# Scoring a key block in one burst of eight matmuls, with one ring of eight PSUM banks for all users

## The chip, the core and the metric

The kernel runs on one core of one Trainium2 chip. The core has a matrix engine (TensorE, called PE in the profile, with its weight loads shown apart as PEld), VectorE (DVE), ScalarE (ACT), GpSimd (POOL), and a queue that only issues transfers (SyncE, SP). PE writes its results to PSUM, which has eight banks; one bank holds 512 fp32 values in each of 128 partitions. ACT and DVE read the banks and write to on-chip memory (SBUF). The metric is the device time of one execution in microseconds, where less is better; the figure given is the median of the runs.

## What is computed

Two parts follow each other. First comes attention over 4 batches, 8 heads, 768 positions and a head size of 64, where each query sees the first 4 keys (the sinks) and the last 128 keys. Then comes a gated feed-forward network (FFN) over all 3072 tokens, 512 wide, with 1536 hidden units and an RMS norm ahead of it. Cut to what matters:

```python
def _attn_ref(q, k, v, n_sink, window):          # B=4, H=8, S=768, D=64, n_sink=4, window=128
    scores = np.matmul(q, k.transpose(0, 1, 3, 2)) / np.sqrt(D)
    keep = (pos[None, :] < n_sink) | ((rel >= 0) & (rel < window))   # rel = query position - key position
    a = softmax(np.where(keep, scores, -1e9))
    return np.matmul(a, v)

def _moe_ref(x, w_gate, w_val, w_out, rms_g):    # x: 3072 x 512, d_ff = 1536
    xn = x / np.sqrt(np.mean(x * x, axis=-1, keepdims=True) + 1e-6) * rms_g
    g = xn @ w_gate
    return (g / (1 + np.exp(-g)) * (xn @ w_val)) @ w_out
```

## The kernel before

The 3072 tokens are 24 blocks of 128, numbered g; block g is position t = g mod 6 of batch b = g div 6. Four blocks make a group G of 512 tokens for the FFN. A key block t is seen by the queries of blocks t and t+1 alone, so the scores are made by key block: for each head one matmul with 128 keys held as weights and 256 queries passing (128 queries at t = 5, the last block of a batch). A head has 64 rows, so these are 64-row matmuls. Two heads, a head pair, stand in the two halves of the 128 rows; a block has four head pairs.

Blocks 0, 1 and 3 are scored by another routine (`unit_bias` and `unit_sp`, L341 and L358): a 128-row matmul first writes the mask into the bank, and eight 64-row matmuls of 128 queries add the scores. The other 21 blocks (2 and 4 to 23) go through `unit_s(g, u)` (L380), called twice for each block. A call scores two head pairs: four 64-row matmuls (L389) into the tile `pT`, which is two banks wide and of which there is one; one exponential on ACT over both banks (L396); and the mask, on DVE (L409) for the first two batches and every first block of a batch, else on POOL (L411, L416). `unit_av(g, u)` (L430) then multiplies the masked exponentials with the values for four heads into a bank `pv`; DVE divides by the sum (L472, L477), ACT squares and sums (L487), and DVE makes the RMS factor and the scaled row `xr` (L496 to L534).

`unit_t1` and `unit_t` (L256, L272) turn queries and keys through PE and a copy on ACT or DVE (from block 12 on, DMAs on SP do it, except for a batch's first block). `unit_x` (L546) does the same for `xr` of the first eight blocks. `unit_sink` and `unit_sink_scores` (L291, L316) do the four sink keys. The FFN is cut into parts: a gate part (four 512-column matmuls into `pg`, then tanh on ACT, L587), a value part (four into `pvl`, then two products on DVE, L592 and L600), and output parts (four each into `po`, three to a bank, then a copy on ACT, L622, and a store from SP). In group 0 a gate or value part is eight matmuls of 256 columns.

The order on PE and SP is the order of the code. `step(g)` (L629) lays the attention work of a block into four slots, and `weave` (L652) deals the slots out between the FFN parts; the first slots of the weave are written by hand (L717 to L729). After the prologue the order on ACT, DVE and POOL is chosen when the program is built, by a scheduler that plans with estimated times. PSUM after the prologue has three rings: `b1` with four banks (FFN, transposes, sinks), `pv` with two (AV), and `pT` with its two. A tile takes the bank of its ring that comes free next in the scheduler's plan, and its first matmul waits on the chip until that bank's last reader is done.

Of the kernel before, what the change touches and what calls it, by code (L numbers as in the profile page):

```python
# [9 lines left out]
ALU = mybir.AluOpType  # L10
ACT = mybir.ActivationFunctionType
FP32 = mybir.dt.float32
BF16 = mybir.dt.bfloat16
# [15 lines left out]
def kernel(  # L29
# [311 lines left out]
    def unit_bias(g, n):  # L341

        if PROLOGUE[0]:
            banks = [pp[0].tile([P, 512], FP32, name="ph", tag="ph", bufs=6)
                     for hi in range(2)]
        else:
            pT = pp[0].tile([P, 2, 512], FP32, name="pT", tag="pT", bufs=1)
            banks = [pT[:, hi, :] for hi in range(2)]
        for hi in range(2):
            nc.tensor.matmul(  # L350
                out=banks[hi].rearrange("p (x c) -> p x c", c=P), lhsT=ident,
                rhs=amasks[:, 0 if g % NT == 0 else 1, n, :].unsqueeze(1).to_broadcast(
                    (P, HP, P)),
                start=True, stop=False, skip_group_check=True,
            )
        PTS[(g, n)] = banks
# [20 lines left out]
            for hp in range(HP):  # L377
                E[(g, 2 * hp + hi, n)] = et[:, hp, :]

    def unit_s(g, u):  # L380
        b, t = divmod(g, NT)
        nq = 2 if t + 1 < NT else 1
        w = nq * P
        pT = pp[0].tile([P, 2, 512], FP32, name="pT", tag="pT", bufs=1)
        for j in range(2):
            hp = 2 * u + j
            for hi in range(2):
                pr = slice(hi * D, (hi + 1) * D)
                nc.tensor.matmul(  # L389
                    out=pT[:, hi, j * 256:j * 256 + w],  # L390
                    lhsT=QKT[b][pr, 1, hp, t * P:(t + 1) * P],
                    rhs=QKT[b][pr, 0, hp, t * P:t * P + w],
                    start=True, stop=True,
                )
        et = epool.tile([P, 4, 2, P], BF16, name="et")
        nc.scalar.activation(  # L396
            out=et[:, :, 0:nq, :].rearrange("p x n c -> p x (n c)"),
            in_=pT.rearrange("p i (j c) -> p (i j) c", c=256)[:, :, 0:w],
            func=ACT.Exp, scale=inv_sqrt_d,
        )  # L400
        if b < POOL_MASK_FROM or t == 0:
            m = masks[:, 0 if t == 0 else 1, 0:nq, :]
            if nq == 2:
                ev = et.rearrange("p x n c -> p x (n c)")
                mv = m.rearrange("p n c -> p (n c)").unsqueeze(1).to_broadcast((P, 4, w))
            else:
                ev = et[:, :, 0, :]
                mv = m.to_broadcast((P, 4, P))
            nc.vector.tensor_tensor(out=ev, in0=ev, in1=mv, op=ALU.mult)  # L409
        else:  # L410
            nc.gpsimd.affine_select(  # L411
                out=et[:, :, 0, :], in_=et[:, :, 0, :], compare_op=ALU.is_ge,
                fill=0.0, base=0, pattern=[[0, 4], [1, P]], channel_multiplier=-1,
            )
            if nq == 2:
                nc.gpsimd.affine_select(  # L416
                    out=et[:, :, 1, :], in_=et[:, :, 1, :], compare_op=ALU.is_ge,
                    fill=0.0, base=-1, pattern=[[0, 4], [-1, P]],
                    channel_multiplier=1,
                )  # L420
        for j in range(2):
            for hi in range(2):
                for n in range(nq):
                    E[(g, 4 * u + 2 * j + hi, n)] = et[:, 2 * hi + j, n, :]

    def halves(g):

# [2 lines left out]
    def unit_av(g, u):  # L430
        b, t = divmod(g, NT)

        pv = pp[0].tile(
            [P, 512], FP32, name="pv", tag="b1" if PROLOGUE[0] else "pv", bufs=2
        )
        if t >= 2:
            nc.tensor.matmul(  # L437
                out=pv[:, 0:HW], lhsT=ESK[(b, t)],
                rhs=VSK[b][:, 4 * u:4 * u + 4, :],
                start=True, stop=False, skip_group_check=True,  # L440
            )
# [223 lines left out]
    with tc.manual_schedule(engines=MANUAL_ALL):  # L665
# [18 lines left out]
        for u in range(2):  # L684
# [16 lines left out]
        )  # L701
        pools.close()
        pp[0] = ctx.enter_context(
            tc.tile_pool(name="psum", bufs=4, space=bass.MemoryType.PSUM)
        )
        PROLOGUE[0] = False

    with tc.manual_schedule(engines=MANUAL):
# [6 lines left out]
        for ft in range(FA, FTN):  # L715
            fb += parts_f(0, (ft,), slice(0, GN))
        weave(fa, [  # L717
            [lambda: unit_t1(2, 1), lambda: unit_bias(1, 1), lambda: unit_sp(1, 1), lambda: unit_sink(0)],
            [lambda: unit_t1(3, 0), lambda: unit_s(2, 0)],
            [lambda: unit_s(2, 1), lambda: unit_sink_scores(0, 2)],  # L720
            [lambda: unit_t1(3, 1), lambda: unit_bias(3, 0), lambda: unit_av(2, 0), lambda: unit_sp(3, 0), lambda: unit_av(2, 1)],
            [lambda: unit_av(3, 0)],
            [lambda: unit_av(3, 1), lambda: unit_t1(4, 0)],
# [2 lines left out]
            [lambda: unit_t1(4, 1)],  # L726
            [lambda: unit_x(3)],
        ], first=True)
        slots = [[lambda: unit_t1(5, 0)], [lambda: unit_s(4, 0), lambda: unit_t1(5, 1)], [lambda: unit_s(4, 1)], [lambda: unit_sink_scores(0, 4)], [lambda: unit_t(6)], []]  # L729
        for g in range(5, NB + 3):  # L730
            slots += step(g)
        slots[6].pop()
# [51 lines left out]
```

## Time and profile before

| | |
|---|---|
| time, median of 3 runs | 261.87 us (261.83, 261.87, 262.98) |
| span of the profiled execution, first to last instruction | 259.7 us |
| median of the runs less that span | 2.2 us |
| instructions in the profile | 4764 |
| PEld, DVE, ACT, POOL busy | 125.8, 180.3, 138.3, 96.6 us |
| mean granted TensorE clock | 0.997 |
| HBM read, written | 28.31 MB, 6.29 MB |

Of the profiled execution only the span is given and no time of its own, so its time is taken as the span and the 2.2 us by which the median of the runs exceeds it. PE's busy time includes the modelled tails of pipelined matmuls, which overlap: a 512-column matmul is shown as 0.379 us, but eight in a row advance by 0.216 us each. How far PE has got is therefore read from the starts of instructions in the timeline and not from busy time. The idle time that the timeline shows in brackets is given with what ended it. Some matmul records are missing (278 of 288 `po` matmuls are there), which shows as an x7 where eight matmuls stand.

### The profile page before, as it was taken

To read this page: it belongs to the slowest core of one execution; us is meant where nothing else is said; L and a number is where in the kernel's file an instruction comes from. 1 tells how busy PE (TensorE), PEld (TensorE's weight loads), DVE (VectorE), ACT (ScalarE), POOL (GpSimd) and SP (SyncE) were. 2 spreads that over 40 slices of the span, in tenths; PEclk is the share of its full clock that TensorE was granted. 3 is DMA by queue.
4 is the path that set the end of the run, shared out by engine and by line. 5 is a ranking of instruction groups with operands and counts; after the bars stand their busy time and mean duration, and the time that the engine had idled before them with its cause. 6 is when DMAs were issued, how large, how long until landed. Compare 5 with 4: busy or idle time off the path is not lost.

```text
span 259.7 us, 4764 instructions
## 1 busy us (share of the span) xinstructions
PE 244.9 (94%) x1733; PEld 125.8 (48%) x1760; DVE 180.3 (69%) x474; ACT 138.3 (53%) x278; POOL 96.6 (37%) x129
## 2 busy tenths in 40 slices
PE   6988989979999999999999997999999999999994
PEld 2536768745545444444454443444444454444441
DVE  5566888797678999438889449788339893177800
ACT  2657666778787464655563643565654442233211
POOL 8996787499996522123122001124222000000000
PEclk9999999999999999999999999999999999999998
DMA  9999999999999999540121550521330112300022
GB/s 130 148 175 189 186 155 195 175 156 148 182 196 164 152 137 99 141 129 14 23 42 23 131 152 6 59 40 24 101 102 3 20 20 61 124 0 0 0 83 81
DMA packets 105849, 25.74 MB, mean 99 GB/s; under 512 B 95073, under 2 KB 102753, under 8 KB 105826
## 3 DMA queue, kind: packets, MB, share of 16 engines
q0 software_dynamic: 80704, 13.90, 72.2%
q1 hardware_dynamic: 24082, 11.28, 19.2%
q10 hardware_dynamic: 1040, 0.26, 0.5%
q8 instruction: 14, 0.23, 0.4%
q14 instruction: 9, 0.07, 0.1%
HBM read 28.31 MB, written 6.29 MB: 133 GB/s over the span
## 4 chain that ended last, share of the span: by engine, by line
PE 82%; DVE 8%; ACT 6%; issue 1%; DMA 1%; ACTq 0%
PE pg L574 23%; PE pvl L574 22%; PE po L615 21%; PE pT L389 4%; PE pqk L251 2%; ACT et L396 2%; PE pv L449 2%; DVE xr L534 1%; PE pv L445 1%; DMA osb<-in_q_dram 1%; PE pss L321 1%; DVE x L477 1%; PE pv L437 1%; DVE hT L600 1%; ACT sq L487 1%
## 5 line engine op out<-in xcount | busy, mean ns | idle before, releaser
L574 PE MATMUL pg<-xnt,wg 128*128 128x512 bf16 (+1 forms) x321 | 73.7, 353 | 2.6 <-DVE p L592 1.7
L574 PE MATMUL pvl<-xnt,wv 128*128 128x512 bf16 (+1 forms) x319 | 73.3, 353 | 0.9 <-ACT xnt L560 0.5
L615 PE MATMUL po<-wo,hT 128*128 128x512 bf16 x278 | 65.7, 379 | 0.5
L592 DVE SCALAR_TENSOR_TENSOR p<-th,pg 128x512 bf16<-128x512 bf16 x72 | 49.1, 682 | 23.6 <-ACT th L587 23.1
L587 ACT ACTIVATE th<-pg 128x512 bf16<-128x512 f32 x72 | 42.7, 594 | 42.0 <-PE pg L574 41.8
L600 DVE TENSOR_TENSOR hT<-p,pvl 128x512 bf16<-128x512 bf16 x72 | 49.3, 685 | 3.4
L411 POOL TENSOR_SCALAR_AFFINE_SELECT et<-et 128x512 bf16<-128x512 bf16 x20 | 12.7, 637 | 87.2 <-ACT et L396 71.7
L396 ACT ACTIVATE et<-pT 128x1024 bf16<-128x1024 f32 (+1 forms) x42 | 39.4, 937 | 10.2 <-PE pT L389 10.2
L574 PEld LDWEIGHTS <-wg 128*128 128x128 bf16 x328 | 29.9, 98 | 28.3 <-issue 4.0
L574 PEld LDWEIGHTS <-wv 128*128 128x128 bf16 x328 | 30.2, 98 | 27.6 <-issue 2.1
L615 PEld LDWEIGHTS <-hT 128*128 128x128 bf16 x288 | 26.4, 98 | 29.6 <-issue 1.5
L487 ACT ACTIVATE sq<-x 128x256 bf16<-128x256 bf16 x48 | 19.9, 414 | 24.3 <-DVE x L477 23.9
L622 ACT ACTIVATE osb<-po 128x512 f32<-128x512 f32 x24 | 14.3, 595 | 28.3 <-PE po L615 24.3
L111 POOL DMA_DIRECT2D qs<-in_q_dram x23 | 20.7, 900 | 8.6 <-DMA ks<-in_k_dram 3.7
L111 POOL DMA_DIRECT2D ks<-in_k_dram x23 | 20.6, 894 | 5.2 <-DMA wo<-in_moe_w_out_dram 2.9
L124 POOL DMA_DIRECT2D v<-in_v_dram x24 | 21.5, 896 | 2.3 <-DMA wg<-in_moe_w_gate_dram 1.4
L472 DVE RECIPROCAL rden<-pv 128x4 f32<-128x4 f32 x48 | 8.4, 176 | 19.1 <-PE pv L449 19.1
L477 DVE TENSOR_TENSOR x<-pv,rden 128x256 bf16<-128x256 f32 x48 | 20.2, 421 | 0.9
L534 DVE SCALAR_TENSOR_TENSOR xr<-x,y,gb 128x512 bf16<-128x512 bf16 (+1 forms) x25 | 19.6, 787 | 0.7
L389 PE MATMUL pT<-qkT 64*128 64x256 bf16 (+1 forms) x168 | 15.6, 264 | 3.0 <-ACT qkT L264 1.5
L409 DVE TENSOR_TENSOR et<-et,masks 128x1024 bf16<-128x1024 bf16 (+1 forms) x22 | 14.1, 640 | 5.7 <-ACT et L396 5.5
L449 PE MATMUL pv<-v,et 128*128 128x65 bf16 x168 | 15.3, 193 | 0.0
(75 smaller groups left out, 212.6 us busy)
## 6 DMA issues: line engine op xcount, KB each, us to landing
out_dram<-osb SPq DMA_DIRECT2D x24, 256.0 KB, 2.2
v<-in_v_dram POOLq DMA_DIRECT2D x24, 128.0 KB, 7.5
qs<-in_q_dram POOLq DMA_DIRECT2D x23, 128.0 KB, 7.4
ks<-in_k_dram POOLq DMA_DIRECT2D x23, 128.0 KB, 7.3
wg<-in_moe_w_gate_dram POOLq DMA_DIRECT2D x6, 256.0 KB, 8.3
wv<-in_moe_w_val_dram POOLq DMA_DIRECT2D x6, 256.0 KB, 8.8
wo<-in_moe_w_out_dram POOLq DMA_DIRECT2D x2, 768.0 KB, 10.4
osb<-in_k_dram ACTq DMA_DIRECT2D x1, 256.0 KB, 4.4
```

Of the source, the lines that this page charges most:

```text
L111: nc.gpsimd.dma_start(out=tl, in_=src[b, :, t * P:(t + 1) * P, :].rearrange("h t d -> t h d"),)
L124: nc.gpsimd.dma_start(out=V16[b][:, t, :, 0:D], in_=v[b, :, t * P:(t + 1) * P, :].rearrange("h t d -> t h d"),)
L389: nc.tensor.matmul(out=pT[:, hi, j * 256:j * 256 + w], lhsT=QKT[b][pr, 1, hp, t * P:(t + 1) * P], rhs=QKT[b][pr, 0, hp, t * P:t * P + w], ...
L396: nc.scalar.activation(out=et[:, :, 0:nq, :].rearrange("p x n c -> p x (n c)"), in_=pT.rearrange("p i (j c) -> p (i j) c", c=256)[:, :, 0: ...
L477: nc.vector.tensor_tensor(out=X16[g][:, heads_of(g, u), :], in0=pvv[:, :, 0:D], in1=RDEN.pop((g, u)).unsqueeze(2).to_broadcast((P, 4, D)), ...
L487: nc.scalar.activation(out=sq, in_=xh, func=ACT.Square, scale=MS_SCALE, accum_out=MS[g][:, u:u + 1],)
L534: nc.vector.scalar_tensor_tensor(out=XR[g][-1], in0=x16[:, c], scalar=y[:, 4:5], in1=gb[:, c], op0=ALU.mult, op1=ALU.mult,)
L574: nc.tensor.matmul(out=ps[:, i * n:(i + 1) * n], lhsT=w_sb[:, kt, ft * P:(ft + 1) * P], rhs=XNT[G][:, kt, cols], start=(kt == 0), stop=(kt ...
L587: nc.scalar.activation(out=st["th"], in_=st["pg"], func=ACT.Tanh, scale=0.5)
L592: nc.vector.scalar_tensor_tensor(out=p1, in0=st["th"], scalar=1.0, in1=st["pg"], op0=ALU.add, op1=ALU.mult,)
L600: nc.vector.tensor_tensor(out=HT[key][:, i:i + n, cols], in0=p1.rearrange("p (n c) -> p n c", n=n), in1=pvl.rearrange("p (n c) -> p n c", ...
L615: nc.tensor.matmul(out=st["po"], lhsT=HT[(G, ft // 2)][:, ft % 2, tb * P:(tb + 1) * P], rhs=wo[:, ft, :], start=(ft == 0), stop=(ft == FTN ...
```

## The change

`unit_s(g)` now scores all four head pairs of a block in one call: eight matmuls in a row, into four single-bank tiles (two at t = 5, where all four pairs of one half fit into one bank). ACT takes the exponential bank by bank, 512 columns at a time, so a block has four exponentials (two at t = 5) in place of two over two banks (two over half as much at t = 5). The masks cover the same elements with the same number of instructions. In `step` the one call stands in slot 0, where the first of the two calls stood; slot 2 loses its call. In the hand-written slots block 2 is scored where its first call stood, and block 4 one slot later, where its second call stood. PSUM after the prologue is one ring of eight banks under the tag `b1`, which all take from: scores, the mask matmuls of `unit_bias`, AV, transposes, sinks, FFN.

```diff
@@ unit_bias
-            pT = pp[0].tile([P, 2, 512], FP32, name="pT", tag="pT", bufs=1)
-            banks = [pT[:, hi, :] for hi in range(2)]
+            banks = [bank() for hi in range(2)]
...
-    def unit_s(g, u):
+    def bank():
+        return pp[0].tile([P, 512], FP32, name="pT", tag="b1")
+
+    def mask(ev, b, t, nq):
...
+    def unit_s(g):
         b, t = divmod(g, NT)
         nq = 2 if t + 1 < NT else 1
         w = nq * P
-        pT = pp[0].tile([P, 2, 512], FP32, name="pT", tag="pT", bufs=1)
-        for j in range(2):
-            hp = 2 * u + j
+        per = 512 // w
+        nb = HP // per
+        banks = [[bank() for hi in range(2)] for u in range(nb)]
+        for hp in range(HP):
+            u, j = divmod(hp, per)
             for hi in range(2):
                 pr = slice(hi * D, (hi + 1) * D)
                 nc.tensor.matmul(
-                    out=pT[:, hi, j * 256:j * 256 + w],
+                    out=banks[u][hi][:, j * w:(j + 1) * w],
                     lhsT=QKT[b][pr, 1, hp, t * P:(t + 1) * P],
                     rhs=QKT[b][pr, 0, hp, t * P:t * P + w],
                     start=True, stop=True,
                 )
-        et = epool.tile([P, 4, 2, P], BF16, name="et")
-        nc.scalar.activation(
-            out=et[:, :, 0:nq, :].rearrange("p x n c -> p x (n c)"),
-            in_=pT.rearrange("p i (j c) -> p (i j) c", c=256)[:, :, 0:w],
-            func=ACT.Exp, scale=inv_sqrt_d,
-        )
...
+        for u in range(nb):
+            et = epool.tile([P, 2, per, nq, P], BF16, name="et")
+            for hi in range(2):
+                nc.scalar.activation(
+                    out=et[:, hi].rearrange("p j n c -> p (j n c)"), in_=banks[u][hi],
+                    func=ACT.Exp, scale=inv_sqrt_d,
+                )
+                if nq == 1:
+                    mask(et[:, hi], b, t, nq)
             if nq == 2:
...
+                mask(et.rearrange("p i j n c -> p (i j) n c"), b, t, nq)
...
@@ unit_av
-        pv = pp[0].tile(
-            [P, 512], FP32, name="pv", tag="b1" if PROLOGUE[0] else "pv", bufs=2
-        )
+        pv = pp[0].tile([P, 512], FP32, name="pv", tag="b1")
@@ step
-            slots[0].append(lambda: unit_s(g, 0))
-            slots[2].append(lambda: unit_s(g, 1))
+            slots[0].append(lambda: unit_s(g))
@@ after the prologue
-            tc.tile_pool(name="psum", bufs=4, space=bass.MemoryType.PSUM)
+            tc.tile_pool(name="psum", bufs=8, space=bass.MemoryType.PSUM)
@@ first weave
-            [lambda: unit_t1(3, 0), lambda: unit_s(2, 0)],
-            [lambda: unit_s(2, 1), lambda: unit_sink_scores(0, 2)],
+            [lambda: unit_t1(3, 0), lambda: unit_s(2)],
+            [lambda: unit_sink_scores(0, 2)],
@@ slots of group 0
-        slots = [[lambda: unit_t1(5, 0)], [lambda: unit_s(4, 0), lambda: unit_t1(5, 1)], [lambda: unit_s(4, 1)], ...]
+        slots = [[lambda: unit_t1(5, 0)], [lambda: unit_t1(5, 1)], [lambda: unit_s(4)], ...]
```

On PE, at the scoring of block 4 (the `pT` rows), the program before has the following order, one row shown of each run of equal matmuls: the turned queries of block 5 (`pqk` from `qs`), two head pairs, the turned keys, a gate part, the other two head pairs, a value part.

```order
L251 MATMUL pqk<-ident,qs 128x128
...
L389 MATMUL pT<-qkT 128x256
...
L251 MATMUL pqk<-ident,ks 128x128
...
L574 MATMUL pg<-xnt,wg 128x256
...
L389 MATMUL pT<-qkT 128x256
...
L574 MATMUL pvl<-xnt,wv 128x256
```

At the same place the changed program has this order:

```order
L251 MATMUL pqk<-ident,qs 128x128
...
L251 MATMUL pqk<-ident,ks 128x128
...
L581 MATMUL pg<-xnt,wg 128x256
...
L413 MATMUL pT<-qkT 128x256
...
L581 MATMUL pvl<-xnt,wv 128x256
```

The keys' transposes and the gate part now stand between the queries' transposes and the first score matmul that needs their copy, and the four `pT` matmuls have become eight in one run.

On ACT, around the scoring of blocks 7 and 8 (`et` rows), the program before has this order; `sq` is the square of an AV half, `qkT` the copy of turned queries and keys, `xnt` of turned `xr` rows, `th` a tanh.

```order
L286 COPY qkT<-pqk 128x8x128
L396 ACTIVATE et<-pT 128x1024
L487 ACTIVATE sq,ms<-x_1050 128x256
L560 COPY xnt<-pxt 128x4x128
L587 ACTIVATE th<-pg 128x512
L396 ACTIVATE et<-pT 128x1024
L487 ACTIVATE sq,ms<-x_1154 128x256
L286 COPY qkT<-pqk 128x8x128
```

At the same place the changed program has this order:

```order
L494 ACTIVATE sq,ms<-x_1072 128x256
L422 ACTIVATE et<-pT 128x512
L567 COPY xnt<-pxt 128x4x128
L594 ACTIVATE th<-pg 128x512
L286 COPY qkT<-pqk 128x8x128
L494 ACTIVATE sq,ms<-x_1180 128x256
L422 ACTIVATE et<-pT 128x512 x3
L494 ACTIVATE sq,ms<-x_1180 128x256
```

The block's exponentials now all stand ahead of the `xnt` copy, the tanh and the `qkT` copy, where half of them stood between; the next block's follow in a run of three.

On ACT in a later stretch, where gate parts run (tanh `th` of L587 before, L594 now), the order before is the following.

```order
L396 ACTIVATE et<-pT 128x1024
L587 ACTIVATE th<-pg 128x512 x2
L487 ACTIVATE sq,ms<-x_2097 128x256
L587 ACTIVATE th<-pg 128x512
L396 ACTIVATE et<-pT 128x1024
L587 ACTIVATE th<-pg 128x512
```

The changed program has this order there:

```order
L494 ACTIVATE sq,ms<-x_2151 128x256
L594 ACTIVATE th<-pg 128x512
L422 ACTIVATE et<-pT 128x512 x4
L594 ACTIVATE th<-pg 128x512
L327 ACTIVATE esk<-pss 128x256
```

A tanh behind the scores now stands behind four exponentials in a row, where one of twice the width stood.

More of the change, by code (lines that the diff above doesn't have):

```diff
@@ L378, in unit_sp @@
                 E[(g, 2 * hp + hi, n)] = et[:, hp, :]
-    def unit_s(g, u):
+    def bank():
+        return pp[0].tile([P, 512], FP32, name="pT", tag="b1")
+    def mask(ev, b, t, nq):
+        x = ev.shape[1]
+        if b < POOL_MASK_FROM or t == 0:
+            m = masks[:, 0 if t == 0 else 1, 0:nq, :]
+            mv = m.rearrange("p n c -> p (n c)").unsqueeze(1).to_broadcast((P, x, nq * P))
+            e = ev.rearrange("p x n c -> p x (n c)")
+            nc.vector.tensor_tensor(out=e, in0=e, in1=mv, op=ALU.mult)
+            return
+        nc.gpsimd.affine_select(
+            out=ev[:, :, 0, :], in_=ev[:, :, 0, :], compare_op=ALU.is_ge,
+            fill=0.0, base=0, pattern=[[0, x], [1, P]], channel_multiplier=-1,
+        )
+        if nq == 2:
+            nc.gpsimd.affine_select(
+                out=ev[:, :, 1, :], in_=ev[:, :, 1, :], compare_op=ALU.is_ge,
+                fill=0.0, base=-1, pattern=[[0, x], [-1, P]],
+                channel_multiplier=1,
+            )
+    def unit_s(g):
         b, t = divmod(g, NT)
@@ L394, in unit_s @@
                 )
[L395 to L424 removed]
+        for u in range(nb):
[4 more added lines that the diff above has]
+                    func=ACT.Exp, scale=inv_sqrt_d,
+                )
+                if nq == 1:
+                    mask(et[:, hi], b, t, nq)
+            if nq == 2:
+                mask(et.rearrange("p i j n c -> p (i j) n c"), b, t, nq)
+            for j in range(per):
+                for hi in range(2):
+                    for n in range(nq):
+                        E[(g, 2 * (u * per + j) + hi, n)] = et[:, hi, j, n, :]
     def halves(g):
@@ L728 @@
         ], first=True)
[L729 removed]
+        slots = [[lambda: unit_t1(5, 0)], [lambda: unit_t1(5, 1)], [lambda: unit_s(4)], [lambda: unit_sink_scores(0, 4)], [lambda: unit_t(6)], []]
         for g in range(5, NB + 3):
```

1 line of the change is left out of this document (removed).

## The prediction

> **What bounds the kernel now.** I read the page first: busy times, the slices, the chain that ended last.
>
> ```profile
> PE 244.9 (94%) x1733; PEld 125.8 (48%) x1760; DVE 180.3 (69%) x474; ACT 138.3 (53%) x278; POOL 96.6 (37%) x129
> PEclk9999999999999999999999999999999999999998
> PE 82%; DVE 8%; ACT 6%; issue 1%; DMA 1%; ACTq 0%
> ```
>
> PE is on the chain for 82% of the span, at full clock, so the end moves by what PE is spared or made to wait. Next I asked what PE waits for, and then for each such place in the timeline.
>
> ```profile
> PE pg L574 <- DVE p L592: 1.7, 1, 1.7
> PE pT L389 <- ACT qkT L264: 1.5, 2, 0.8
> PE pT L389 <- ACT qkT L286: 1.4, 2, 0.9
> PE pvl L574 <- ACT xnt L560: 0.5, 1, 0.5
> ```
> ```profile
> 36.99 0.39 PE L389 MATMUL pT<-qkT 64*128 64x256 bf16 x4 [0.84 <-ACT qkT L264]
> 54.16 0.40 PE L389 MATMUL pT<-qkT 64*128 64x256 bf16 x4 [0.86 <-ACT qkT L286]
> 56.59 1.02 PE L574 MATMUL pvl<-xnt,wv 128*128 128x512 bf16 x4 [0.49 <-ACT xnt L560]
> 72.55 0.39 PE L389 MATMUL pT<-qkT 64*128 64x256 bf16 x4 [0.52 <-ACT qkT L286]
> 161.52 1.02 PE L574 MATMUL pg<-xnt,wg 128*128 128x512 bf16 x4 [1.68 <-DVE p L592]
> ```
>
> The reader is to see how few and short PE's waits are: after the first 30 us only these five matter, four of them for ACT between 36 and 73 us, one for DVE at 161 us. The engines' load by stretch says why they lie there.
>
> ```profile
> core 0: us, PE busy (x) PEld busy (x) DVE busy (x) ACT busy (x) POOL busy (x), PEclk, DMA share, GB/s
> 36.00:63.00 27.00, 24.69 (x254) 16.98 (x254) 22.41 (x61) 20.54 (x38) 21.09 (x25) 1.00 2.16 169
> 63.00:76.00 13.00, 12.37 (x114) 6.63 (x114) 8.99 (x32) 10.72 (x22) 12.06 (x15) 1.00 2.47 176
> 76.00:100.00 24.00, 23.79 (x163) 11.31 (x165) 22.22 (x56) 13.80 (x30) 11.34 (x13) 1.00 2.14 157
> ```
>
> From 36 to 76 us, where group 0 runs and attention for blocks 4 to 10 stands between few FFN parts, ACT is busy 31.3 of 40 us. Later ACT has room (13.8 of 24), and there DVE is the fuller one (22.2 of 24).
>
> **First term: one burst in place of two.** What a burst of scores costs PE is read from what stands around it.
>
> ```profile
> 103.00 1.89 PE L615 MATMUL po<-wo,hT 128*128 128x512 bf16 x8
> 104.82 0.39 PE L389 MATMUL pT<-qkT 64*128 64x256 bf16 x4
> 105.15 1.04 PE L615 MATMUL po<-wo,hT 128*128 128x512 bf16 x4
> L615 PE MATMUL po<-wo,hT 128*128 128x512 bf16 x278 | 65.7, 379 | 0.5
> L389 PE MATMUL pT<-qkT 64*128 64x256 bf16 x136 | 13.3, 273 | 3.0 <-ACT qkT L264 1.5 <-ACT qkT L286 1.4
> L389 PE MATMUL pT<-qkT 64*128 64x128 bf16 x32 | 2.3, 221 | 0.0
> ```
>
> Eight `po` matmuls last 1.89 us, of which the last one's shown length is 0.379, so they advance by (1.89 - 0.379) / 7 = 0.216 us. After 8 x 0.216 = 1.73 us, at 104.73, the next `po` could have begun; it began at 105.15. A burst of four score matmuls therefore costs 0.42 us. Its parts: the first score matmul starts 0.09 late; the last starts 0.39 - 0.273 = 0.12 after it (the two heads of a pair start together, so this is the pitch of a pair); 0.21 us pass from there to the next 128-row matmul. The first and the third part, less 0.12 for the last pair's own columns, 0.18 us in all, are paid for each change between 64-row and 128-row matmuls and back.
>
> In a burst of eight, two more pairs at 0.12 give 0.66 us, against 2 x 0.42 = 0.84: 0.18 us less for a block. That later pairs don't pay the change again is shown by the one routine that already runs eight 64-row matmuls in a row, and the short burst of a t = 5 block stands beside it, with the AV half ahead of it.
>
> ```profile
> 31.23 0.59 PE L350 MATMUL pT<-amasks,ident 128*128 128x512 bf16 x2
> 31.76 0.41 PE L365 MATMUL pT<-qkT 64*128 64x128 bf16 x8
> 32.10 1.05 PE L574 MATMUL pvl<-xnt,wv 128*128 128x256 bf16 x8
> 140.76 0.27 PE L437 MATMUL pv<-vsk,esk 128*128 128x260 bf16 x1
> 141.11 1.89 PE L615 MATMUL po<-wo,hT 128*128 128x512 bf16 x8
> 142.94 0.28 PE L389 MATMUL pT<-qkT 64*128 64x128 bf16 x4
> 143.15 1.04 PE L615 MATMUL po<-wo,hT 128*128 128x512 bf16 x4
> ```
>
> Eight of 128 columns cost 32.10 - 31.23 - 2 x 0.216 = 0.44 us, four of them 143.15 - 141.11 - 1.73 = 0.31: again 0.62 - 0.44 = 0.18 less. The trace has (136 + 32) / 4 = 42 bursts, hence 21 blocks, and 21 x 0.18 = 3.8 us. No row shows eight of 256 columns; between nothing saved (each later pair pays the change again) and 0.21 (a pair advances like a 256-column matmul, half of 0.216) I take 0.18. [...]
>
> **Second term: the wait at 161.52.** That gate part takes a bank of a ring of four whose reader, a product on DVE, came late.
>
> ```profile
> 159.33 0.39 PE L306 MATMUL pvs<-v,sel 128*128 128x260 bf16 x2
> 160.79 0.68 DVE L592 SCALAR_TENSOR_TENSOR p<-th,pg 128x512 bf16<-128x512 bf16 x1
> ```
>
> The product ended at 161.47, and PE went on at 161.52. In the changed program this gate part takes a bank of block 19's scores, free after the second exponential. PE needs a gate part (4 x 0.216 = 0.86), a value part, the two `pvs` and an AV half between, some 2.2 us, and two exponentials need 1.2 (row below); the wait goes, and the products get later banks without PE at their heels. Worth 1.7 us; nothing if DVE's lag finds another bank.
>
> **Third term: blocks 4 to 10, where ACT has little room.**
>
> ```profile
> L396 ACT ACTIVATE et<-pT 128x1024 bf16<-128x1024 f32 x34 | 34.7, 1019 | 9.6 <-PE pT L389 9.6
> L396 ACT ACTIVATE et<-pT 128x512 bf16<-128x512 f32 x8 | 4.7, 589 | 0.6 <-PE pT L389 0.6
> L587 ACT ACTIVATE th<-pg 128x512 bf16<-128x512 f32 x72 | 42.7, 594 | 42.0 <-PE pg L574 41.8
> L592 DVE SCALAR_TENSOR_TENSOR p<-th,pg 128x512 bf16<-128x512 bf16 x72 | 49.1, 682 | 23.6 <-ACT th L587 23.1
> ```
>
> Four exponentials of 512 columns take 4 x 0.589 = 2.36 us where two of 1024 took 2.04: 0.32 us more on ACT for each block, except the four at t = 5. In this stretch that is six blocks, 1.9 us. All four waits there end with ACT's release, so I charge ACT's work to the end. For it: seven blocks' bursts, 7 x 0.18 = 1.3 us, and the wait at 36.99, whose 0.84 goes, since the block is now scored behind a gate part of 0.86. Together 1.3 + 0.8 - 1.9 = +0.2 us gained. The two rows of order on ACT say where it shows: the `qkT` copy that releases the next block's scores stands behind all four exponentials, so the waits like those at 54.16 and 72.55 stay or grow, while DVE's work is the same. Ends: all four waits and the bursts gained, 2.7 + 1.3 = 4.0 us; or the copies late by a further 0.32 for every block, 0.2 - 1.9 = -1.7.
>
> Elsewhere the extra ACT time is hidden behind PE (ACT 13.8 of 24). The masks and their engines stay. The scores of a block's second half come a half step sooner, and AV asks for them a step later, so nothing waits for them; SP's and POOL's transfers keep their order. In the first 36 us I count block 2's burst alone. **The sum:** bursts of block 2 and blocks 11 to 23, 14 x 0.18 = 2.5; the wait at 161, 1.7; blocks 4 to 10, 0.2: 4.4 us. The profiled execution's span of 259.7 becomes 255.3; the runs' median lies 2.2 above that span, and with the same 2.2 the time is 257.5 us.
>
> **The rivals.** *The early stretch runs free:* with eight banks PE meets no wait between 36 and 76 us. That is 4.0 in place of 0.2, a gain of 8.2 and 253.7 us. Against it stand ACT's 31.3 of 40 us, and copies that queue behind the exponentials.
>
> *The change doesn't do what it says:* the four banks come free one by one, so that the burst stops in its midst, or each pair pays the change. Then 2.5 goes from the sum, and 1.9 is left: 260.0 us. For it: four of eight banks must be free at once. Against it: the planner gives the scores banks that were taken about eight allocations before, some 5 us of PE.
>
> *Waits on banks eat the bursts:* scores, AV and the FFN now share one ring, and each of blocks 11 to 23 waits about as much as its burst saves, 0.2 us: 2.5 lost, 260.0; with the wait at 161 kept as well, 261.7.
>
> *Slower: the tanh behind four exponentials.* A gate part that ends as the scores do has its tanh behind 2.36 us of exponentials; with the tanh's 0.594 and the product's 0.682 its bank is free 3.63 us after. Until PE asks for that bank, eight allocations on, it has some five FFN parts and two AV halves (141.11 - 140.76 = 0.35 each, by the rows at 140.76), 5 x 0.86 + 2 x 0.35 = 5.0 us. It decides when DVE has over 1.4 us queued ahead of that product: two masks and an `xr` (rows below) are 2.2 us, a wait of 0.8. If nine of blocks 11 to 23, those that run beside gate parts, meet it, 7.2 us are lost: 264.7 us.
>
> ```profile
> L409 DVE TENSOR_TENSOR et<-et,masks 128x1024 bf16<-128x1024 bf16 x18 | 12.4, 689 | 5.7 <-ACT et L396 5.5
> L534 DVE SCALAR_TENSOR_TENSOR xr<-x,y,gb 128x512 bf16<-128x512 bf16 x23 | 18.7, 813 | 0.7
> ```
>
> For it: DVE's 22.2 of 24 us. Against it: most masks of those blocks are POOL's.
>
> *The clock drops.* Before, single waits of up to 1.68 us left it at full rate; only the start is slower.
>
> ```profile
> 1.26 2.74 PE L335 MATMUL pw<-idle 128*128 128x512 bf16 x6 [1.26 <-DVE idle L102]
> ```
>
> Six matmuls in 2.74 us advance by about 0.43, twice 0.216; every 10 us in that state would cost 5, so one such stretch more than undoes the sum: 262.5 us. [...]
>
> **How the numbers follow.** Forecast, ACT-bound early and free later: 0.53. Early stretch free as well: 0.17. Burst not held: 0.07. Bank waits eat the bursts: 0.13, half of it at 260.0 and half at 261.7. Tanh chain: 0.08. Clock: 0.02. The forecast's own range is 255.8 (half of the early waits gone) to 259.2 (the stretch at its bad end of -1.7). The range must reach to 260.4, to take in the burst that isn't held and the milder bank waits, and down to 254.4, most of the way to the free early stretch; it leaves out some 2 in 10. A measurement here can tell about 0.5%, or 1.3 us, from no change. Faster by more than that, under 260.6: 0.53 + 0.17, most of 0.07 and half of 0.13, 0.82. Within it: 0.09. Slower: 0.08 and a little for the clock, 0.09.
>
> **What would show it right or wrong.** Bursts: 21 runs of eight at L413, with 0.66 us between the 128-row work around them; about 0.84 refutes the first term. The wait for DVE's product near 157 us should be gone from PE's waits. PE's waits for the `qkT` copy should stand between 45 and 72 us in about the old sum; none there means 254, more than 4 us there means that ACT took the gain. ACT busy should be some 5 us up (17 blocks x 0.32) and DVE and POOL unchanged. Gate parts that wait for L599 or L607 behind each block would mean the tanh chain, and a slice of PEclk below 9 in the middle the clock.

## The result, and the profile after

The changed kernel takes 254.59 us, the median of 4 runs (254.02 to 255.25), against 261.91 us for the kernel before in the same comparison (4 runs): a ratio of 0.971, with a 95% interval of 0.969 to 0.974. Run once more unchanged, it took 255.40 us (5 runs, 255.20 to 255.56) against 261.77 us (17 runs): 0.975, 0.972 to 0.977. So the change saves 6.4 to 7.3 us, where the prediction had 4.4. The profiled execution's span is 252.6 us (its own time 254.38), 7.1 less than before.

From the page of the changed kernel: the busy times, the granted clock by slices, the chain that ended last by engine.

```profile
PE 238.8 (95%) x1733; PEld 127.4 (50%) x1760; DVE 181.1 (72%) x474; ACT 139.6 (55%) x312; POOL 98.1 (39%) x129
PEclk9999999999999999999999999999999999999999
PE 67%; DMA 12%; DVE 8%; POOL 7%; ACT 2%; issue 2%; POOLq 0%; ACTq 0%; DVEq 0%
```

PE is spared 6.1 us of busy time, and the clock holds. New is the chain: transfers (DMA) and the engine that issues them (POOL) have 19% of it, which before had 1% for DMA. What PE waits for says the same; here are the rows of the changed kernel's wait list (total, times, longest) that have a wait of 0.19 us or more after the first 30 us:

```profile
PE pqk L251 <- DMA qs<-in_q_dram: 1.3, 2, 0.7
PE pxt L563 <- DVE xr L541: 1.3, 3, 0.7
PE pqk L251 <- DMA ks<-in_k_dram: 1.0, 2, 0.6
```

The wait for DVE's product is gone, and so is every wait for the copy of turned queries and keys at L286. In their place PE waits for loads of queries and keys. The timeline of PE in the changed kernel (in brackets the idle time of PE and what ended it) has them at blocks 5 and 8:

```profile
35.11 0.40 PE L251 MATMUL pqk<-ident,qs 128*128 128x128 bf16 x4 [0.72 <-DMA qs<-in_q_dram]
35.95 0.40 PE L251 MATMUL pqk<-ident,ks 128*128 128x128 bf16 x4 [0.45 <-DMA ks<-in_k_dram]
50.68 0.40 PE L251 MATMUL pqk<-ident,qs 128*128 128x128 bf16 x4 [0.61 <-DMA qs<-in_q_dram]
51.65 0.40 PE L251 MATMUL pqk<-ident,ks 128*128 128x128 bf16 x4 [0.58 <-DMA ks<-in_k_dram]
```

Three pieces of the chain in order of time (start, duration) show why block 8's loads are late: POOL issues them behind the two loads of the output weights, and the keys take 12.47 us to land, where the median of all loads of keys is 7.7.

```profile
36.66 1.64 POOL wo L142 x2
38.31 0.84 POOL qs L111
39.14 12.47 DMA ks<-in_k_dram
```

The burst can be read as before, from the output matmuls around it:

```profile
103.66 1.89 PE L622 MATMUL po<-wo,hT 128*128 128x512 bf16 x7
105.49 0.61 PE L413 MATMUL pT<-qkT 64*128 64x256 bf16 x8
106.03 2.33 PE L622 MATMUL po<-wo,hT 128*128 128x512 bf16 x10
```

The first row's 1.89 us is that of eight (one record is missing), so the next `po` could have begun at 103.66 + 8 x 0.216 = 105.39; it began at 106.03. A burst of eight costs 0.64 us, and a block saves 2 x 0.42 - 0.64 = 0.20. Seven more bursts of eight between 88 and 172 us, read in the same way, cost 0.64 us each.

**A ledger.** The FFN parts come in the same order in all the programs here, so the start of the first weight load of the same part can be compared from trace to trace. The table has the start before and, for each kernel, how much later (+) or earlier (-) the part begins; the other columns belong to the experiments below.

| FFN part | before, us | after | after again | e1 | e2 | e3 | e5 | e10 |
|---|---|---|---|---|---|---|---|---|
| A, first gate part | 17.27 | -1.04 | -1.27 | +0.29 | +0.53 | +0.08 | -1.19 | -1.23 |
| B, value part | 34.25 | -1.76 | -1.99 | +0.28 | -0.18 | -0.64 | -1.91 | -1.95 |
| C, value part behind block 8's transposes | 51.86 | -0.03 | +0.84 | +0.98 | -0.20 | +0.58 | -2.05 | +0.63 |
| D, value part | 76.27 | -2.28 | -1.41 | 0.00 | -0.64 | -1.41 | -3.63 | -1.62 |
| E, gate part | 159.65 | -4.19 | -3.31 | -0.19 | -2.27 | -3.32 | -5.54 | -3.53 |
| F, value part | 162.17 | -6.03 | -5.16 | -2.04 | -2.01 | -5.16 | -7.38 | -5.37 |
| G, last output part | 253.02 | -7.11 | -6.24 | -2.11 | -1.61 | -6.25 | -8.46 | -6.45 |

Three things can be read from the columns of the changed kernel. From D to E and from F to G, 13 blocks are scored, and 1.91 + 1.08 = 2.99 us are saved in small steps. From E to F, 1.84 us go at once: the wait of before at 161.52. And ahead of D nothing adds up simply: 1.0 to 1.3 us are there before the first part that the change touches, and they are lost again at C, the part behind the wait for block 8's keys.

### The profile page after: what moved, and what is told of

The parts are those of the page before. It is cut to its first block, busy times and chain, and to the rows that moved or that the text cites. A ratio compares the mean times of both kernels' runs of the same rounds, so it can differ in the third digit from the quotient of the medians.

```text
span 252.6 us, 4804 instructions
## 1 busy us (share of the span) xinstructions
PE 238.8 (95%) x1733; PEld 127.4 (50%) x1760; DVE 181.1 (72%) x474; ACT 139.6 (55%) x312; POOL 98.1 (39%) x129
## 4 chain that ended last, share of the span: by engine, by line
PE 67%; DMA 12%; DVE 8%; POOL 7%; ACT 2%; issue 2%; POOLq 0%; ACTq 0%; DVEq 0%
PE po L622 23%; PE pvl L581 18%; PE pg L581 18%; DMA wv<-in_moe_w_val_dram 7%; DMA ks<-in_k_dram 5%; PE pT L413 3%; DVE p L599 2%; POOL v L124 2%; POOL qs L111 2%; DVE hT L607 2%; PE pv L456 1%; PE pv L452 1%; PE pv L444 1%; POOL ks L111 1%; ACT et L422 1%
## 5 line engine op out<-in xcount | busy, mean ns | idle before, releaser
L622 PE MATMUL po<-wo,hT 128*128 128x512 bf16 x279 | 64.9, 379 | 0.5 <-issue 0.2
L594 ACT ACTIVATE th<-pg 128x512 bf16<-128x512 f32 x72 | 42.9, 596 | 39.1 <-PE pg L581 39.0
L422 ACT ACTIVATE et<-pT 128x512 bf16<-128x512 f32 x76 | 39.8, 602 | 4.8 <-PE pT L413 4.6
L456 PE MATMUL pv<-v,et 128*128 128x65 bf16 x168 | 15.3, 193 | 0.0
L452 PE MATMUL pv<-v,et 128*128 128x65 bf16 x136 | 12.7, 193 | 0.0
```

Source lines behind the costliest of these rows:

```text
L422: nc.scalar.activation(out=et[:, hi].rearrange("p j n c -> p (j n c)"), in_=banks[u][hi], func=ACT.Exp, scale=inv_sqrt_d,)
L456: nc.tensor.matmul(out=dest, lhsT=E[(g, h, 0)], rhs=V16[b][:, t, h, :], start=(t == 0), stop=True, skip_group_check=True,)
L594: nc.scalar.activation(out=st["th"], in_=st["pg"], func=ACT.Tanh, scale=0.5)
L622: nc.tensor.matmul(out=st["po"], lhsT=HT[(G, ft // 2)][:, ft % 2, tb * P:(tb + 1) * P], rhs=wo[:, ft, :], start=(ft == 0), stop=(ft == FTN ...
```

## Experiments

My theory after the result: the bursts and the ring of eight do what the prediction says, but between 34 and 52 us it is the loads of queries and keys that PE runs into, not ACT. The main rival keeps the prediction's view, that ACT's work there is charged to the end.

**e1, the bursts undone, the ring kept.** `unit_s` is called twice again, each call filling two single banks:

```diff
-            slots[0].append(lambda: unit_s(g))
+            slots[0].append(lambda: unit_s(g, 0))
+            slots[2].append(lambda: unit_s(g, 1))
```

> The ring of eight and the exponentials of 512 columns stay; the scores of a block stand again in two bursts of four, where the kernel before had them (t = 5 blocks keep their one burst, as they fill two banks only). Theory 1 (two parts that add up: a saved burst is worth 0.20 us, and the ring of eight alone takes the wait of 1.7 us near 160 us away): 17 blocks x 0.20 = 3.4 us over the changed kernel's 254.6, so about 258.0, without a PE wait for DVE's product L592/L599 near 160. Theory 2 (the ring does nearly all, bursts are worth nothing): 254.1 to 255.1. Theory 3 (the ring does nothing by itself, all comes with the burst): 259.8 or more, with the wait near 160 back.

Measured: 259.49 us (6 runs), 0.992 of before (0.990 to 0.994). The wait near 160 us stays away (E to F: -1.85), so the ring removes it without the bursts, and theory 3 falls. From D to G, without that wait, e1 has lost 2.99 - 0.26 = 2.73 us against the changed kernel, over the 10 blocks there that are not t = 5: 0.27 a block, a little over the 0.20 expected. The total is 1.5 above theory 1, which is thus incomplete: with two bursts PE's waits for ACT's copies are back, and of the waits for loads only one, of 0.56 us, is left. From e1's wait list:

```profile
PE pT L418 <- ACT qkT L264: 1.6, 2, 0.9
PE pT L418 <- ACT qkT L286: 1.0, 2, 0.7
```

The timeline of ACT shows how. First before, then e1, at the copy that block 7's scores wait for:

```profile
51.80 1.02 ACT L396 ACTIVATE et<-pT 128x1024 bf16<-128x1024 f32 x1
52.70 0.42 ACT L487 ACTIVATE sq<-x 128x256 bf16<-128x256 bf16 x1
53.10 1.01 ACT L286 COPY qkT<-pqk 128x1024 bf16<-128x1024 bf16 x1
```
```profile
52.02 0.59 ACT L427 ACTIVATE et<-pT 128x512 bf16<-128x512 f32 x1
52.60 0.42 ACT L499 ACTIVATE sq<-x 128x256 bf16<-128x256 bf16 x1
53.02 0.58 ACT L427 ACTIVATE et<-pT 128x512 bf16<-128x512 f32 x1
53.49 1.00 ACT L286 COPY qkT<-pqk 128x1024 bf16<-128x1024 bf16 x1
```

And the changed kernel at the same copy:

```profile
48.79 1.57 ACT L422 ACTIVATE et<-pT 128x512 bf16<-128x512 f32 x3
50.23 0.63 ACT L594 ACTIVATE th<-pg 128x512 bf16<-128x512 f32 x1
52.09 1.01 ACT L286 COPY qkT<-pqk 128x1024 bf16<-128x1024 bf16 x1 [1.23 <-PE pqk L251]
```

Before and in e1, the second burst's exponentials fall just ahead of the copy. In the changed kernel all four were done by 50.36 us, because their matmuls stand half a step earlier, and ACT stood idle for 1.23 us until PE had turned the keys. They are ahead of the copy in the order, but not in its way. Nearly all of that idle time comes from the late loads, though: PE had waited 0.61 and 0.58 us for them before it turned the keys (rows at 50.68 and 51.65). How little room ACT has without them is shown at e5.

**e2, the bursts kept, the ring split.** Four banks for scores, masks and AV, four for the rest:

```diff
-        return pp[0].tile([P, 512], FP32, name="pT", tag="b1")
+        return pp[0].tile([P, 512], FP32, name="pT", tag="pT", bufs=4)
...
-            tc.tile_pool(name="psum", bufs=8, space=bass.MemoryType.PSUM)
+            tc.tile_pool(name="psum", bufs=4, space=bass.MemoryType.PSUM)
```

> The bursts of eight stay; the eight banks are split: four for scores, the mask matmuls of unit_bias and AV, four for the FFN, transposes and sinks, as many as these had before. Theory 1 (the wait near 160 us came from the FFN's ring of four): it comes back, 254.6 + 1.8 = 256.4, and more where a burst must wait until DVE has read the AV bank, at most the AV's norm chain of about 1 us for some of the 21 blocks, so 256.4 to 265. Theory 2 (only the burst counts, the ring was just room for its four banks): 254.1 to 255.1.

Measured: 258.78 us (6 runs), 0.989 (0.986 to 0.992). The wait is back, and in this profile it costs more than its length. PE's timeline in e2 at that place, and the row of the table by stretch (busy times of PE, PEld, DVE, ACT, POOL, then the granted clock, DMA share, GB/s):

```profile
159.51 1.18 PE L582 MATMUL pg<-xnt,wg 128*128 128x512 bf16 x4 [1.94 <-DVE p L600]
160.48 1.91 PE L582 MATMUL pvl<-xnt,wv 128*128 128x512 bf16 x4
162.19 1.76 PE L582 MATMUL pg<-xnt,wg 128*128 128x512 bf16 x4
163.78 1.03 PE L582 MATMUL pvl<-xnt,wv 128*128 128x512 bf16 x4
```
```profile
160.24:163.66 3.42, 3.42 (x10) 1.22 (x9) 2.28 (x6) 1.11 (x3) 0.00 (x0) 0.50 0.68 95
```

The eight matmuls from 160.48 to 163.78 take 3.30 us, where eight that advance by 0.216 take 1.73, as the granted clock is at half rate there (0.50 in the row). That this is part of e2's median is not shown: two of its six runs have a mean clock of 0.993, as this profile has, and take 258.26 and 259.79 us; the other four have 0.999 or 1.000 and take 258.27 to 259.64. The split has a second cost that e2 was not meant to test: scores and AV now share four banks, and bursts wait for these. From e2's wait list:

```profile
PE pT L413 <- DVE x L485: 0.9, 2, 0.6
PE pT L413 <- ACT et L422: 0.6, 1, 0.6
```

These waits lie between 48 and 61 us; from C to D e2 gains 0.44 us on the kernel before, where the changed kernel gains 2.25. Without the ring the bursts are worth 3.0 us, the ring without the bursts 2.3, both together 6.4 to 7.3: each removes waits that the other leaves, and bursts of eight wait for banks where scores and AV have only four.

**e3 and e6, more work for ACT.** For each of blocks 4 to 10, one exponential more (e3) or three more (e6), into a tile that nobody reads:

```diff
+            if u == 0 and 4 <= g <= 10:
+                more = epool.tile([P, 512], BF16, name="more", bufs=2)
+                nc.scalar.activation(
+                    out=more, in_=banks[0][0], func=ACT.Exp, scale=inv_sqrt_d,
+                )
```

> The changed kernel with one exponential more on ACT (128x512, 0.60 us, into a tile that nobody reads) for each of blocks 4 to 10, ahead of what follows there. Theory A (as predicted: ACT's work in the stretch from 36 to 76 us is charged to the end): 7 x 0.60 = 4.2 us more, about 258.8, with PE waits for the copies qkT L264/L286. Theory L (there PE waits for the loads of the q and k blocks and ACT has slack): 254.1 to 255.6, and PE's waits stay those for qs and ks.

> The changed kernel with three exponentials more for each of blocks 4 to 10, 7 x 3 x 0.49 (the pitch of exponentials in a row) = 10.3 us of ACT time, against 7.0 us that ACT idles between 36 and 76 us in the changed kernel. Theory L with a slack of that size: it costs 3.3 us or more, 258 to 262, and PE's waits for the copies L264/L286 and xnt come back. Theory S (the slack is larger, since the scheduler moves other work of ACT out of the stretch): 254.8 to 256.5.

Measured: e3 255.22 us (6 runs), as the changed kernel run again (255.40); e6 260.83 us (12 runs). One exponential a block costs nothing that can be told: with the loads as they are, ACT isn't what this stretch waits for, and theory A falls. (The same test with the loads in time was not run.) Three cost 5.4 us, against r1, of the 10.3 added, so some 5 us of ACT's time were free there, and then the waits that the prediction had in mind do come. From e6's wait list:

```profile
PE pT L413 <- ACT qkT L286: 3.6, 4, 1.6
PE pg L587 <- ACT xnt L573: 1.8, 2, 1.3
```

**r1, the changed kernel again.**

> The changed kernel once more, unchanged. Theory P (the start differs from execution to execution): its first gate part begins at 17.3 to 17.8 us, as in the five other profiles, not at 16.22, and the qs and ks waits near 35 and 51 us are shorter by about as much as PE comes later; the span is 252.6 to 253.7. Theory C (the early start belongs to the changed program): 16.2 us again and a span of 252.6 or less.

Measured: 255.40 us, span 253.4. Its first gate part came even earlier than in the first profile (15.99 us), which speaks for theory C, and yet its span is 0.8 longer, which neither theory had. The rows say why: for the transposes of block 8's keys, first r1, then e3 (a start 1.35 us later), then e10 (below):

```profile
52.52 0.40 PE L251 MATMUL pqk<-ident,ks 128*128 128x128 bf16 x4 [0.58 <-DMA ks<-in_k_dram]
```
```profile
52.26 0.40 PE L251 MATMUL pqk<-ident,ks 128*128 128x128 bf16 x4 [0.56 <-DMA ks<-in_k_dram]
```
```profile
52.31 0.40 PE L251 MATMUL pqk<-ident,ks 128*128 128x128 bf16 x4 [0.57 <-DMA ks<-in_k_dram]
```

From this row to the end of the span it is 200.9 us in r1 (253.4 - 52.52), 201.1 in e3, 201.0 in e10 and 201.0 in the first profile (252.6 - 51.65). Where block 8's keys land sets the end, whether the program began early or late. The first profile was the shortest because its keys landed first.

What differs at the start is the clock. The first transposes of before, then of r1:

```profile
5.01 0.61 PE L251 MATMUL pqk<-ident,qs 128*128 128x128 bf16 x4 [1.01 <-DVE qs L174]
```
```profile
5.18 0.40 PE L251 MATMUL pqk<-ident,qs 128*128 128x128 bf16 x4 [1.19 <-DVE qs L174]
```

Of the ten profiles of programs with six matmuls at the start, three (both of the changed kernel, and e5) have the 0.40 us of full rate here: they reach full rate at 4.2 to 4.7 us, by the clock recorded in the traces. The other seven, of both kinds of program, have 0.61 and reach it at 8.9 to 10.1 us. In e3, e4 and e6, which share the changed program's start, it is 0.61, so theory C falls: the early start is chance.

**e4 and e5, the loads moved.** Block 8's q, k and v ahead of the output weights in both; block 5's q and k ahead of the last weight chunk (e4) or right behind it (e5, shown):

```diff
         load_w(5)
+        load_q(5)
+        load_k(5)
         load_v(4)
+        load_v(5)
-        for g in range(GB + 1, 2 * GB):
+        for g in range(GB + 2, 2 * GB):
...
+        load_q(8)
+        load_k(8)
+        load_v(8)
         load_wo(0)
...
```

> The changed kernel with two moves in the order of the loads: block 5's q and k ahead of the last chunk of the gate and value weights, block 8's q, k and v ahead of the two loads of the output weights. Theory L (loads are what the early stretch waits for): the four PE waits for qs and ks near 35 and 51 us, some 3.0 us together, go; 251.6 if nothing takes their place, and over 253 if half comes back as waits for the delayed weights. Theory A (ACT is next at once): the waits turn into waits for the copies L264/L286, and the time stays 254.1 to 255.1.

> The changed kernel with block 5's q and k loaded right behind the last weight chunk (only block 4's v moves behind them) and block 8's q, k and v ahead of the output weights' two loads. Theory L (loads are what the early stretch waits for, and the last weight chunk isn't needed as early as in e4_loads): the waits for block 8's qs and ks go, block 5's shrink to 0 to 0.5 us, the wait of 0.5 us for the gate weights that e4_loads showed is absent: 253.0 to 253.8. Rival (e4_loads already had all there is): 253.6 to 254.6.

Measured: e4 253.77 us, e5 253.87 us (6 runs each). In e5, block 8's transposes no longer wait:

```profile
49.42 0.39 PE L257 MATMUL pqk<-ident,qs 128*128 128x128 bf16 x4
49.64 0.39 PE L257 MATMUL pqk<-ident,ks 128*128 128x128 bf16 x4
```

That is worth 0.7 to 0.8 us against the first median of the changed kernel and 1.5 to 1.6 against the second. It is less than the sum of the four waits for loads (2.4 us in the first profile, 3.5 in r1; the 3.0 in e4's expectation is neither), as part comes back: in e5 two waits of 0.28 and 0.56 for block 5 stay, and one of 0.51 for DVE is new; e4 has that one too (0.52), and a new one of 0.23 for the `xnt` copy. The wait of 0.46 at the first gate part, which e4's profile puts down to a transfer, is not new: all the profiles have 0.46 to 0.52 us there, and the others put it down to the `xnt` copy.

With the loads in time, ACT comes close to mattering. Its timeline in e5, at the copy for block 7's scores:

```profile
48.31 1.57 ACT L428 ACTIVATE et<-pT 128x512 bf16<-128x512 f32 x3
49.74 0.63 ACT L600 ACTIVATE th<-pg 128x512 bf16<-128x512 f32 x1
50.22 1.05 ACT L292 COPY qkT<-pqk 128x1024 bf16<-128x1024 bf16 x1
```

The copy follows the tanh at once. PE had turned the keys by 50.03 (49.64 + 0.39), so exponentials and tanh hold the copy up by some 0.2 us; PE's scores begin at 51.33, just after its end at 51.27. After the first 21 us, e5's wait list has no wait for ACT.

Theory A (no gain over the changed kernel) falls with e4. Between e4 and e5 no difference can be told, so e5's rival, that e4 had all there is, may be right. By the profiles e4's order is even ahead from part A on: it gains 8.07 us from A to G (+0.33 and -7.74) and e5 7.27; but e4 began late and e5 early. e4's order with the start of e7 was not run.

**e7, r2 and e10, a surer start.** Nine matmuls in place of six in `unit_warm` at the start: with e5's loads (e7, repeated as r2), and alone (e10).

> As e5_loads_v4_later, with nine matmuls in place of six that keep TensorE busy at the very start, until about the time (5.1 us) when the first transposes can begin. Theory W (the clock reaches full rate after a stretch of unbroken work): the transposes near 5 us are at full pitch (0.06 us apart rather than 0.11), the first gate part begins near 16.3 us, and 0.5 to 1.1 us is saved against e5_loads_v4_later. Rival (the clock's rise does not depend on it): the first gate part at 17.3 us or later, no gain.

> e7_loads_warm once more. Theory W (nine matmuls make the early clock sure): first gate part near 16.0 us again and 252.4 to 253.4. Rival (its start was chance, as that of e5_loads_v4_later's profile may have been): 17.3 us in this profile, or a median over 253.4.

> The changed kernel with nine matmuls in place of six at the start and the loads in their old order. Theory L (PE gets to the transposes of blocks 5 and 8 before their loads land, so an early start only makes those waits longer): first gate part near 16.1 us, waits for qs and ks of 2.8 us or more together, and 254.6 to 255.5, as the changed kernel; with the loads moved as well the same nine matmuls gave 0.7 to 1.0 us. Rival (the early start is kept, whatever the loads do): 253.6 to 254.4.

Measured: e7 252.90 us (6 runs, 252.40 to 253.17), 0.965 of before (0.962 to 0.968); r2 253.17 us (5 runs), 0.968 (0.965 to 0.971); their first gate parts begin at 16.04 and 16.34 us. e10 began as early (16.03) and took 255.19 us (5 runs): alone, the early start is lost at the loads, as theory L has it; its waits for queries sum to

```profile
PE pqk L251 <- DMA qs<-in_q_dram: 2.1, 2, 1.5
```

where the first profile had 1.3. With the loads moved the early start is kept, for 0.7 to 1.0 us over e5. e7 is the best version here, by its two medians 1.4 to 2.5 us ahead of the changed kernel.

**e8 and e9, the same two edits in the kernel before.**

> The kernel before with the order of loads of e5_loads_v4_later, and nothing else. Theory L (the wait for the loads came up only because the changed kernel reaches those transposes earlier; before, PE waited for ACT's copies there): within 0.5 us of the kernel before, 261.3 to 262.3, with the waits for L264, L286 and xnt as they were. Rival (the loads held the kernel before too, so the new order is worth as much in both): 260.0 to 260.8.

> The kernel before with that order of loads and nine matmuls at the start, as e7_loads_warm has them; against e7_loads_warm's 252.9 it gives what the change is worth when both programs start alike and neither waits for those loads. By the ledger of e7_loads_warm's profile (8.4 us, of which 1.2 stand before the first gate part) that is 7.2 us: 260.1, and 0.7 to 1.2 us less than e8_before_loads if nothing gives the early start back. Rival (ACT's waits near 37 and 54 us take the early start back): 261.3 or more.

Measured: e8 262.06 us (12 runs), 1.001 of before (0.998 to 1.003); e9 260.69 us (12 runs), 0.996 (0.994 to 0.997). In e8, PE waits for the same copy as before, and the loads don't matter:

```profile
54.77 0.39 PE L395 MATMUL pT<-qkT 64*128 64x256 bf16 x4 [0.86 <-ACT qkT L292]
```

So the wait for loads is one that the change brought to light. Between e9 and e7 the change is worth 260.69 - 252.90 = 7.8 us (7.5 against r2): that is its size when both programs have nine matmuls at the start and block 8's loads are in time. The 7.2 expected was somewhat low, as was the 260.1 for e9.

## Why the prediction was right or wrong, step by step

**What bounds the kernel.** PE, at full clock: right, but for the stretch up to 52 us of the changed kernel, where the loads do. The 2.2 us by which a time was taken to exceed its span was high: the profiled executions that have a time of their own exceed theirs by 1.7 to 1.9.

**First term, the bursts.** Right in mechanism. The burst of eight costs 0.64 us where 0.66 was estimated. A block at t = 5 saves as much: its one burst costs 0.43 us, two cost 2 x 0.31. For blocks 11 to 23, 2.3 us were counted and 2.99 saved: 13 x 0.20 = 2.6, and 0.4 in small steps that I haven't traced to a cause.

**Second term, the wait for DVE's product.** Right: 1.84 us against 1.7. e1 has the ring without the bursts and no wait; e2 has a ring of four for the FFN, and the wait is back with 1.94.

**Third term, blocks 4 to 10: this is the step that failed.** It said: "All four waits there end with ACT's release, so I charge ACT's work to the end", and that the waits for the `qkT` copy "stay or grow". They went, all of them, and e3 shows that ACT's work is not charged. Two errors stand behind it. The rows of order say what stands ahead of the copy on ACT, and I took that for what delays it; the timeline shows that the four exponentials end 1.7 us before the copy begins (50.36 and 52.09), mostly because of the late loads, and that with the loads in time (e5) they and the tanh hold the copy up by only some 0.2 us. And the price of 0.32 us a block was added up from durations that overlap: three exponentials in a row take 1.57 us, hence advance by (1.57 - 0.59) / 2 = 0.49, so four take 3 x 0.49 + 0.59 = 2.06, against the 2.04 that stood for two of 1024 columns. Those overlap as well (the row at 51.80 of before is followed after 0.90), so something is left: ACT's busy time rose by 1.3 us, or 0.08 for each of 17 blocks, not by 5.

What took the waits' place was on no list of mine: PE came sooner to the transposes of blocks 5 and 8 than their loads. I had noted that the transfers keep their order, and not asked whether they were still in time. The loads thus took back much of what the bursts and the copies gave: from A to D the changed kernel gained 1.24 us in the first profile and 0.14 in r1, and e5, with block 8's loads in time, 2.44. Up to D, the early start by chance included, it gained 2.28 and 1.41 us, against the 0.4 that I counted. (In e3, which began late, it is 1.41 as well: the landing of block 8's keys sets it.) The difference is 1.9 and 1.0 us, the larger part of the 2.7 and 1.8 by which the ledger's 7.11 and 6.24 exceed the predicted 4.4; the bursts' 0.65 and the wait's 0.14 are the rest.

That the term's 0.2 us lies among what was measured for its stretch is luck: from B to D the first profile gained 0.52 us and r1 lost 0.58, where waits that I expected went and waits that I had not thought of came. With block 8's loads in time it is 1.72 (e5), still short of the 4.0 of the term's good end.

**The first 36 us.** I counted one burst, 0.18. From A to B it is 0.72 in both profiles of the changed kernel and in e3, and nothing in e1: short waits from block 2's second burst to block 3's scores went with the second burst.

**The rivals.** The early stretch running free (253.7) was nearest to the truth, but for the loads; with the loads moved, e5 comes to 253.87. That the two figures agree is partly luck, as the rival's 4.0 us for blocks 4 to 10 is more than e5 gained there and the other terms were counted too low. The rival of a burst not held took off only 2.5 us: the 1.3 us of bursts inside the third term would have gone as well. And the 255.8 at the good end of the forecast's own range does not follow from half of the early waits: half of 2.7 us gives 256.2. In the changed kernel no burst of blocks 4 to 23 stops in its midst, none of blocks 11 to 23 waits for a bank, and no tanh chain shows. The clock held (a mean of 1.00 in the profiled execution).

## What to carry to other kernels

A wait that goes shows what was waiting behind it: before counting a gain, set the new arrival time of PE against the landing time of each load in that stretch, and not only against the engines. Whether an instruction is in another's way is read from its start and end beside the other's start, not from the order on the engine, and the time of a run of instructions from their starts, not from the sum of their durations. And where a gain or a chance start is swallowed at one fixed point, compare programs from that point on.

## What the runs showed of the hardware

In e2, 1.94 us of idle time on PE were followed by 3.42 us at half rate, while before 1.68 us at the same place left it at full rate. e9 has a second such fall: 3.41 us at half rate from 14.47 us on, with no idle time of PE above 0.70 us near it. Here are the rows by stretch: e2's 3.41 us ahead of its fall, e9's 3.41 us ahead of its fall and the fall, and the 3.41 us around the wait of before.

```profile
156.83:160.24 3.41, 1.47 (x12) 0.86 (x11) 3.34 (x6) 0.98 (x3) 2.52 (x4) 1.00 0.04 8
```
```profile
11.06:14.47 3.41, 2.71 (x20) 1.18 (x20) 2.98 (x14) 2.16 (x9) 3.34 (x6) 1.00 1.89 170
14.47:17.88 3.41, 3.05 (x15) 1.51 (x13) 1.79 (x7) 1.61 (x4) 2.52 (x5) 0.50 1.97 174
```
```profile
159.16:162.57 3.41, 1.73 (x13) 0.92 (x12) 3.34 (x8) 0.16 (x1) 0.91 (x2) 1.00 0.15 28
```

The same kind of wait thus costs 1.7, or 1.9 and some 1.6 more. Both falls last about as long (3.42 and 3.41 us); what sets that length is not shown. Nor is it shown what decides whether the clock falls. It isn't PE's busy time in the 3.41 us ahead alone: 1.47 us in e2 and 2.71 in e9 were followed by a fall, and 1.73 us around the wait of before by none.

At the start, six matmuls (2.74 us) from 1.26 us on gave full rate by the first transposes (5.2 to 5.4 us) in three profiles of ten, and otherwise at 8.9 to 10.1 us; with nine (3.6 to 4.0 us) all four profiles had it by 5.7 us (e9's fell once more, as above, and its first gate part came at 17.2; of e9's twelve runs only this one and one more, its two longest, have a mean clock of 0.993). The point of change moves: it lies between 4.22 and 5.65 us with nine matmuls and in the three early starts with six, and in e5 and e9 it came 2.96 and 2.97 us after the first matmul. In the three with six it came after the last of these had ended (1.26 + 2.74 = 4.00 us), while PE stood idle. What sets the point is not shown. In these fourteen profiles six matmuls left the early clock to chance and nine were enough; four profiles with nine don't make it sure.
